# Gate and up products of a linear-attention block: another product carries a tail, other forms of x keep it, and W is loaded and summed in another order

## The chip, the cores and the metric

The kernel runs on one core of a Trainium2 chip. The metric is device time in microseconds, from launch to end, of one execution; lower is better. The engines are named as the profile names them: PE (matrix multiply) with PEld (its weight loads), DVE (vector), ACT (scalar, activation functions), POOL (gpsimd) and SP, which here only issues DMAs. Each engine runs its own instructions in program order, and so does each engine's DMA queue: a DMA that has to wait keeps back those behind it.

## The reference

One block of float32 work on x of 2048 rows and 576 columns: a layer norm, a linear attention with 32 heads, and a gated feed-forward of width 4608 that gates it.

```python
xn = layernorm(x)
s  = linear_attention(xn, wqkv) @ wo
g  = xn @ w_gate                     # 2048 x 4608
u  = xn @ w_up                       # 2048 x 4608
b  = (gelu(g) * u) @ w_down          # 2048 x 576
out = x + s * silu(b)
```

## The kernel before

All products are made from words: a float32 operand is cut into a high word (a rounding to `float32r`, made by a copy on ACT) and a low word (operand minus high word, made by a subtraction on DVE), and a product is the sum of three passes, high by high, high by low and low by high.

**Stages.** Keys and values of row tiles 0 to 7 (`kv_tile`) and the q products of the first half of x (`q_store`, to about 107 us), the same for tiles 8 to 15 and the second half (to about 220), the attention's output s (`s_mm`, to about 287), gate and up (`matrix`, to about 1087), and the down product (`down_all`, to the end). Work of one stage is prepared in the gaps of the stage before by lists of closures (`behind`, `ahead`, `aside`) that run after a numbered tile.

**Gate and up.** There are 36 matrices W of 576 x 256, gate and up in turn, each multiplied by all of x. Rows of x come in four blocks of 512 (two halves `s` of the sequence with two blocks `b` each), and W, without its last 64 of the 576 inputs, in 2 x 2 quarters of 256 x 128. A 2 x 2 product is made from seven products instead of eight, with sums of quarters of W (`S1` to `S4`, `mat_sums` on POOL) and of x (`T1` to `T4`, formed once). They come in this order, with the PSUM name that each adds into:

| number | 0 | 1 | 2 | 3 | 4 | 5 | 6 |
|---|---|---|---|---|---|---|---|
| PSUM | al | be | ga | de | al | ga | de |
| W | A11 | S2 | S1 | S3 | A12 | S4 | A22 |
| x | B11 | T2 | T1 | T3 | B21 | B22 | T4 |

The last 64 inputs are the *tail*. It isn't part of the scheme of seven: four products carry one plain tail product each, of 64 rows of W (`wtail`, cut from `raw[q][:, 4]`) with 64 rows of x that stand in slot 2 of a form of x. Before, they are number 3 (tail of T3), 4 (T1), 5 (T3) and 6 (T2, whose tail is that of block 0 minus that of block 1, so that what number 3 put into `de` is taken out again).

**Two halves of each product.** PE's rows are used as two groups of 64. The early half of a product pairs the lower 64 rows for `s = 1` with the upper 64 for `s = 0`, the late half the other way about. `step` (line 996) issues the early half of a product, then the sums and cuts that belong two products back (`post_0` to `post_6`, each followed by the list `todo[i]`), then the late half of the product before. So the order on PE is E0 L6 E1 L0 E2 L1 E3 L2 E4 L3 E5 L4 E6 L5, where L6 belongs to the matrix before. A half has 12 matmuls; a tail makes it 14 (early) or 16 (late). `act(seen ...)` reads a PSUM bank after each early half, which ties ACT's order to PE's. The rows of the profile call forms of x that were built in place for `s = 1` `xo_T`, `xo_B`, and those kept in HBM and loaded back for `s = 0` (`keep`, `back`) `xr_T`, `xr_B`.

**W.** `raw[q]` is one buffer (640 KB). In matrix q the words of matrix q + 1 are cut: A11 in `todo[0]`, S1 to S3 in `todo[3]`, A12, A22 and the tail in `todo[4]`, S4 in `todo[5]`; right behind the cuts of `todo[4]` SP is given the load of W of q + 2. `mat_sums(q + 1)` is given to POOL ahead of the whole matrix q.

**Results of gate and up.** Four matrices make a macro step of 28 hooks (`HOOKS`, one per product). Products land in 17 spots of SBUF; POOL adds them up by the hand-written table `ADDS` (sum, two terms, sign, hook), and finished ones are stored to HBM on SP one hook later (`put_out`; the last macro stores on POOL). A spot is used again once its store has landed. These run from `run_events`, the last entry of each `todo[i]`.

**The way into the down stage** is given by `down_first`, spread over the `todo` lists of the last matrix: loads of weights into the buffers `REG` ("22" into 13, "42" into 7), words of them (`w_head`, and `w_end` in 11), and loads of the first stored results (`raw_a` in buffer 15, which held the words `wa`, and `raw_b` in 10). Buffer 7 held T2 and 8 held T1 for `s = 0` (`X_BACK`), 11 T2 and 10 T3 for `s = 1` (`X_SLOT`).

**Forms of x.** `form("T1")`, `form_apart("T3")`, `form("T2")` and a begun `T4` make those for `s = 0` during the q products and the first tiles after them; `build` makes those for `s = 1` during `s_mm`. `tail` fills slot 2; for T2 it subtracts two blocks on DVE (`xd`), copies on ACT and subtracts on DVE, twice.

Of the kernel before, what the change touches and what calls it, by code (L numbers as in the profile page):

```python
# [8 lines left out]
F32 = mybir.dt.float32  # L9
# [7 lines left out]
P = 128  # L17
# [78 lines left out]
TAIL = {"T1": (0,), "T3": (1,), "T2": (0, 1)}  # L96
# [6 lines left out]
def block_kernel(ctx, tc, x, xe, xt, wq_d, wkv_d, wo, wgu_d, wd_d, out):  # L103
# [69 lines left out]
    small = sb.tile([P, 640], F32, name="small")  # L173
# [174 lines left out]
    def kept_words(nm, o):  # L348

        if nm in TAIL:  # L350
            return o.rearrange("p k t -> p (k t)")
        return bass.AP(
            tensor=o.tensor, offset=o.offset, ap=[list(o.ap[0]), [3 * TBN, 2], [1, 2 * TBN]]
        )

    def kept_place(nm, d):

        if nm in TAIL:
# [3 lines left out]
    def kept(s, nm):  # L362
        store[s, nm] = d = dr.tile(
            [P, 5 if nm in TAIL else 4, TBN], F32, name=f"kept_{s}_{nm}"
# [11 lines left out]
    def tail(s, nm, o):  # L376

        h = s * TR
        for j in range(2):
            vs = [xf[s][BS[b][j]][:, 2, :] for b in TAIL[nm]]  # L380
            r, low = (slice(i + j * KR, i + (j + 1) * KR) for i in (h, TR - h))
            v = vs[0][r]
            if len(vs) == 2:
                d = tmp([P, TBN], f"xd_{s}_{j}")
                vec("tensor_sub", d[r], v, vs[1][r])
                v = d[r]
            act(o[r], v, AF.Copy)
            vec("tensor_sub", o[low], v, o[r].bitcast(F32))
# [4 lines left out]
    def form_lo(s, nm, o):  # L393
        vec("tensor_sub", o[:, 3:5], xf[s][nm][:, 0:2], o[:, 0:2].bitcast(F32))
        if nm in TAIL and (s, nm) not in store:
            tail(s, nm, o[:, 2, :])

    def build(s, nm, i):
        xo[s][nm] = o = big(i, [P, 5, TBN], F32R, f"xo_{s}_{nm}")
# [516 lines left out]
    def mat_sums(q):  # L916
        if q >= NQ:
            return
        rv = raw[q][:, 0:4].rearrange("p (j k) (f c) -> p j f k c", j=2, f=2)
        a11, a21, a12, a22 = rv[:, 0, 0], rv[:, 0, 1], rv[:, 1, 0], rv[:, 1, 1]  # L920
        sm = mid(2, [P, 4, 2, P], F32, f"sm_{q}")
# [4 lines left out]
        sums[q] = rv, sm  # L926
# [6 lines left out]
    def cut_tail(q):  # L933
        o, src = wt["tail", q % 2], raw[q][:, 4, :]
# [9 lines left out]
    def mat_pieces(q):  # L944
# [3 lines left out]
        rv, sm = sums.pop(q)  # L948
        if q % 2 == 0:
            raws_ = [lambda: cut_w(wt["b"][:, 1:3], rv[:, 1])]  # L950
        else:
            raws_ = [
                lambda: cut_w(wt["b"][:, 1:2], rv[:, 1, 0:1]),
                lambda: cut_w(wt["b"][:, 0:1], rv[:, 1, 1:2]),
            ]
        raws_.append(lambda: cut_tail(q))
        return [
            [lambda: cut_w(wt["a"][:, 0:1], rv[:, 0, 0:1])],
            [], [],
            [lambda: cut_w(wt["a"][:, 1:4], sm[:, 0:3])],  # L960
            raws_,
            [lambda: cut_w(wt["b"][:, 3:4], sm[:, 3:4])],
# [52 lines left out]
    def matrix(q, c22, done, todo):  # L1015

        u, bs = {}, {}
        wtail = wt["tail", q % 2]

        def tail_of(f, nm):  # L1020
            c = slice(f * P, (f + 1) * P)
# [824 lines left out]
```

## Time and profile before

| | us |
|---|---|
| median of three runs | 1476.9 (1473.81 to 1477.27) |
| the profiled execution, its own time | 1477.23 |
| its span, first to last instruction | 1475.4 |
| mean granted clock of PE | 0.992 of full speed |

The profile is of that one execution. Its page gives busy times and the costliest groups; the trace behind it can be asked for waits (who stood still, and what ended it), for the chain of work that ended last, for a timeline of one engine and for windows. In a row "a<-b,c" the first name is what is written. "[2.56 <-DMA hs<-spot_h]" behind a row is the idle time ahead of it and what ended it. Ends of matmuls are modelled, and durations on POOL are rough.

### The profile page before, as it was taken

The numbers are of one execution on the slowest core, as the hardware profiler recorded it, in microseconds if no ns is written. First come the engines' busy times: TensorE is split into PE (matmuls) and PEld (weight loads), VectorE is DVE, ScalarE is ACT, GpSimd is POOL, SyncE is SP. The second block draws the span as 40 slices with busy tenths as digits, with TensorE's granted clock in tenths as the row PEclk, the third lists the DMA queues.
The fourth block names the chain that finished last, engine by engine and source line by source line (L and its number), as shares of the span: only waits on it lengthen the run. The fifth ranks groups of instructions, "written<-read, shape, count | busy, mean of one in ns | idle before, by whom it ended". The sixth has DMA issues, their size and how long they took to land.

```text
span 1475.4 us, 29114 instructions
## 1 busy us (share of the span) xinstructions
PE 1441.6 (98%) x11656; PEld 1299.7 (88%) x11656; DVE 993.8 (67%) x1491; ACT 574.5 (39%) x1217; POOL 515.5 (35%) x520
## 2 busy tenths in 40 slices
PE   9998999999999999999999999999979999999998
PEld 8988988999988788887888888888779999999998
DVE  7687667344665555566554565655658987989888
ACT  6444365333222332322333322333225546455454
POOL 3341340114564547556364664538423000000000
PEclk9999999999999999999999999999989999999999
DMA  5545105522323314324242332324169888767886
GB/s 221 174 164 168 44 10 177 189 101 80 134 100 108 122 57 155 101 90 143 66 144 76 136 104 103 128 75 145 68 224 350 280 254 258 237 189 240 278 287 218
DMA packets 120594, 228.68 MB, mean 155 GB/s; under 512 B 11690, under 2 KB 45386, under 8 KB 119690
## 3 DMA queue, kind: packets, MB, share of 16 engines
q1 hardware_dynamic: 117530, 214.82, 43.8%
q0 software_dynamic: 2784, 11.80, 2.2%
q8 instruction: 92, 1.51, 0.4%
q14 instruction: 44, 0.36, 0.1%
q10 hardware_dynamic: 144, 0.20, 0.0%
HBM read 145.20 MB, written 81.53 MB: 154 GB/s over the span
## 4 chain that ended last, share of the span: by engine, by line
PE 85%; DVE 6%; DMA 5%; ACT 2%; issue 1%; POOL 1%; SPq 0%; ACTq 0%; DVEq 0%; POOLq 0%
PE bd L152 23%; PE de L152 15%; PE al L152 13%; PE ga L152 13%; PE kv L152 8%; PE be L152 5%; PE s L152 3%; DMA hs<-spot_h 2%; PE q L152 2%; DVE wb L149 1%; PE kv_a L152 1%; DVE xo_T L149 1%; DMA xr_B<-kept_B 1%; DVE raw_h L149 0%; DVE sx L149 0%
## 5 line engine op out<-in xcount | busy, mean ns | idle before, releaser
L155 POOL TENSOR_TENSOR sm<-raw 128x256 f32<-128x256 f32 x72 | 53.1, 737 | 287.3 <-DMA raw<-in_wgu_dram 247.2
L152 PE MATMUL de<-xr_T,wa 64*128 64x512 f32 x540 | 140.7, 388 | 5.4 <-DVE spot_h L149 3.5
L152 PE MATMUL de<-xo_T,wa 64*128 64x512 f32 x540 | 141.9, 388 | 0.0
L152 PE MATMUL de<-xo_T,wb 64*128 64x512 f32 x540 | 139.7, 386 | 0.0
L152 PE MATMUL de<-xr_T,wb 64*128 64x512 f32 x540 | 139.7, 386 | 0.0
L152 PE MATMUL kv<-wkv,xo_B 128*128 128x412 f32 (+2 forms) x662 | 127.0, 351 | 4.8 <-ACT xo_B L146 4.8
L152 PE MATMUL ga<-xr_T,wa 64*128 64x512 f32 x486 | 127.7, 387 | 0.0
L152 PE MATMUL ga<-xo_T,wa 64*128 64x512 f32 x486 | 127.7, 387 | 0.0
L152 PEld LDWEIGHTS kv<-wkv,xo_B 128*128 128x128 f32 x662 | 121.8, 190 | 6.6 <-ACT xo_B L146 5.4
L152 PE MATMUL bd<-w_head,hi 128*128 128x288 f32 x516 | 119.3, 298 | 8.2 <-ACT hi L146 8.2
L149 DVE TENSOR_TENSOR wa<-raw,wa 128x256 fp32r<-128x256 f32 x54 | 43.1, 799 | 114.8 <-ACT wa L146 114.8
L152 PEld LDWEIGHTS de<-xr_T,wa 64*128 64x128 f32 x540 | 98.8, 184 | 16.6 <-DVE spot_h L149 6.0
L152 PE MATMUL ga<-xo_B,wb 64*128 64x512 f32 x432 | 110.1, 387 | 3.2 <-DVE spot_m L149 3.2
L152 PE MATMUL al<-xr_B,wb 64*128 64x512 f32 x432 | 110.6, 389 | 1.7 <-DMA xr_B<-kept_B 1.7
L152 PE MATMUL al<-xo_B,wb 64*128 64x512 f32 x432 | 110.6, 389 | 0.0
L152 PE MATMUL ga<-xr_B,wb 64*128 64x512 f32 x432 | 110.0, 388 | 0.1
L152 PE MATMUL al<-xr_B,wa 64*128 64x512 f32 x432 | 109.5, 386 | 0.0
L152 PE MATMUL al<-xo_B,wa 64*128 64x512 f32 x432 | 109.5, 386 | 0.0
L152 PE MATMUL be<-xr_T,wa 64*128 64x512 f32 x432 | 109.4, 386 | 0.0
L152 PE MATMUL be<-xo_T,wa 64*128 64x512 f32 x432 | 109.4, 386 | 0.0
L152 PEld LDWEIGHTS de<-xo_T,wb 64*128 64x128 f32 x540 | 99.4, 184 | 9.4
L152 PEld LDWEIGHTS de<-xo_T,wa 64*128 64x128 f32 x540 | 98.8, 184 | 9.6
(297 smaller groups left out, 4596.1 us busy)
## 6 DMA issues: line engine op xcount, KB each, us to landing
raw_h<-hs SPq DMA_DIRECT2D x176, 256.0 KB
raw<-in_wgu_dram SPq DMA_DIRECT2D x36, 640.0 KB
hs<-spot_h SPq DMA_DIRECT2D x90, 256.0 KB
hs<-spot_g SPq DMA_DIRECT2D x80, 256.0 KB
b<-in_wd_dram SPq DMA_DIRECT2D x42, 432.0 KB
hs<-spot_m SPq DMA_DIRECT2D x38, 256.0 KB
raw_g<-hs SPq DMA_DIRECT2D x22, 256.0 KB
raw_a<-hs SPq DMA_DIRECT2D x20, 256.0 KB
```

The lines of the kernel that those rows point to most:

```text
L149: pin(getattr(nc.vector, op)(*args, **kw))
L152: pin(nc.tensor.matmul(*args, **kw))
L155: pin(getattr(nc.gpsimd, op)(*args, **kw))
```

## The change

Tails: number 2 (`ga`, S1 with T1) now carries the second half of the W tail with block 1's tail of x, number 3 carries none, number 4 the first half with block 0's tail, number 5 the difference of the two W halves with block 1's, and number 6 the second half with block 0's. All are plain tails of x; the difference is now on the side of W: `mat_sums` makes one more subtraction on POOL (128 x 128), and `cut_two` cuts it into two words (`wt["last"]`, in the buffer that `small` had). Block 0's tail is kept in T4 for both halves of the sequence; block 1's in T1 (`s = 0`) and T3 (`s = 1`). So T4 and T1 are now stored and loaded with five slots for `s = 0`, and T2 and T3 with four.

Order: `mat_sums(q + 1)` moves from ahead of matrix q to the head of `todo[0]`, its sums live in one lasting tile, and the load of W of q + 2 moves from the end of the cuts in `todo[4]` to the end of `todo[5]`, behind that list's events. At the start B21 is loaded back ahead of W of matrix 1 instead of behind it. For `s = 1` block 0's tail is made beside T1 as before, but into T4, whose buffer is opened earlier.

```diff
@@ -93,7 +93,7 @@
 
 MAIN = ((0, 0), (0, 2), (2, 0), (1, 1), (1, 3), (3, 1))
 XW = (0, 1, 3, 4)
-TAIL = {"T1": (0,), "T3": (1,), "T2": (0, 1)}
+TAIL = ({"T4": 0, "T1": 1}, {"T4": 0, "T3": 1})
 TR = P // 2
 
 X_SLOT = {"B11": 0, "B21": 1, "B22": 3, "T1": 9, "T3": 10, "T2": 11, "T4": 2}
@@ -170,7 +170,7 @@
     ident = sb.tile([P, P], F32, name="ident")
     make_identity(nc, ident)
     eps_t, zx, seen = eps_t[:, 0:1], eps_t[:, 2:3], eps_t[:, 4:6]
-    small = sb.tile([P, 640], F32, name="small")
+    small = sb.tile([P, 640], F32, tag="small", bufs=1, name="small")
     nc.gpsimd.memset(eps_t, LN_EPS)
 
 
@@ -347,7 +347,7 @@
 
     def kept_words(nm, o):
 
-        if nm in TAIL:
+        if nm in TAIL[0]:
             return o.rearrange("p k t -> p (k t)")
         return bass.AP(
             tensor=o.tensor, offset=o.offset, ap=[list(o.ap[0]), [3 * TBN, 2], [1, 2 * TBN]]
@@ -355,13 +355,13 @@
 
     def kept_place(nm, d):
 
-        if nm in TAIL:
+        if nm in TAIL[0]:
             return d.rearrange("p k t -> p (k t)")
         return d.rearrange("p (a b) t -> p a (b t)", a=2)
 
     def kept(s, nm):
         store[s, nm] = d = dr.tile(
-            [P, 5 if nm in TAIL else 4, TBN], F32, name=f"kept_{s}_{nm}"
+            [P, 5 if nm in TAIL[0] else 4, TBN], F32, name=f"kept_{s}_{nm}"
         )
         return d
 
@@ -373,30 +373,30 @@
         d = kept(s, nm)
         dma(out=kept_place(nm, d), in_=kept_words(nm, o.bitcast(F32)))
 
-    def tail(s, nm, o):
+    def tail(s, b, o):
 
         h = s * TR
         for j in range(2):
-            vs = [xf[s][BS[b][j]][:, 2, :] for b in TAIL[nm]]
+            v = xf[s][BS[b][j]][:, 2, :]
             r, low = (slice(i + j * KR, i + (j + 1) * KR) for i in (h, TR - h))
-            v = vs[0][r]
-            if len(vs) == 2:
-                d = tmp([P, TBN], f"xd_{s}_{j}")
-                vec("tensor_sub", d[r], v, vs[1][r])
-                v = d[r]
-            act(o[r], v, AF.Copy)
-            vec("tensor_sub", o[low], v, o[r].bitcast(F32))
+            act(o[r], v[r], AF.Copy)
+            vec("tensor_sub", o[low], v[r], o[r].bitcast(F32))
 
     def form_hi(s, nm, o):
         act(o[:, 0:2], xf[s][nm][:, 0:2], AF.Copy)
 
     def form_lo(s, nm, o):
         vec("tensor_sub", o[:, 3:5], xf[s][nm][:, 0:2], o[:, 0:2].bitcast(F32))
-        if nm in TAIL and (s, nm) not in store:
-            tail(s, nm, o[:, 2, :])
+        if nm in TAIL[s] and nm != "T4":
+            tail(s, TAIL[s][nm], o[:, 2, :])
+
+    def begin(s, nm, i):
+        xo[s][nm] = big(i, [P, 5, TBN], F32R, f"xo_{s}_{nm}")
 
     def build(s, nm, i):
-        xo[s][nm] = o = big(i, [P, 5, TBN], F32R, f"xo_{s}_{nm}")
+        if nm not in xo[s]:
+            begin(s, nm, i)
+        o = xo[s][nm]
         form_hi(s, nm, o)
         form_lo(s, nm, o)
         return o
@@ -916,14 +916,21 @@
     def mat_sums(q):
         if q >= NQ:
             return
-        rv = raw[q][:, 0:4].rearrange("p (j k) (f c) -> p j f k c", j=2, f=2)
+        rv = quarters(q)
         a11, a21, a12, a22 = rv[:, 0, 0], rv[:, 0, 1], rv[:, 1, 0], rv[:, 1, 1]
-        sm = mid(2, [P, 4, 2, P], F32, f"sm_{q}")
+        if not sums:
+            t = mid(2, [P, 9, P], F32, "sums")
+            sums["sm"] = t[:, 0:8].rearrange("p (s f) c -> p s f c", f=2)
+            sums["last"] = t[:, 8]
+        sm = sums["sm"]
         pool("tensor_add", sm[:, 0], a21, a22)
         pool("tensor_sub", sm[:, 1], sm[:, 0], a11)
         pool("tensor_sub", sm[:, 2], a11, a21)
         pool("tensor_sub", sm[:, 3], a12, sm[:, 1])
-        sums[q] = rv, sm
+        pool("tensor_sub", sums["last"], raw[q][:, 4, 0:P], raw[q][:, 4, P:])
+
+    def quarters(q):
+        return raw[q][:, 0:4].rearrange("p (j k) (f c) -> p j f k c", j=2, f=2)
 
     def cut_w(o, src):
 
@@ -931,7 +938,9 @@
         vec("tensor_sub", o[:, :, 2:4, :], src, o[:, :, 0:2, :].bitcast(F32))
 
     def cut_tail(q):
-        o, src = wt["tail", q % 2], raw[q][:, 4, :]
+        cut_two(wt["tail", q % 2], raw[q][:, 4, :])
+
+    def cut_two(o, src):
         act(o[:, 0], src, AF.Copy)
         vec("tensor_sub", o[:, 1], src, o[:, 0].bitcast(F32))
 
@@ -945,21 +954,25 @@
 
         if q >= NQ:
             return [[] for _ in range(7)]
-        rv, sm = sums.pop(q)
-        if q % 2 == 0:
-            raws_ = [lambda: cut_w(wt["b"][:, 1:3], rv[:, 1])]
-        else:
-            raws_ = [
-                lambda: cut_w(wt["b"][:, 1:2], rv[:, 1, 0:1]),
-                lambda: cut_w(wt["b"][:, 0:1], rv[:, 1, 1:2]),
-            ]
-        raws_.append(lambda: cut_tail(q))
+
+        def raws_(q=q):
+            rv = quarters(q)
+            if q % 2 == 0:
+                cut_w(wt["b"][:, 1:3], rv[:, 1])
+            else:
+                cut_w(wt["b"][:, 1:2], rv[:, 1, 0:1])
+                cut_w(wt["b"][:, 0:1], rv[:, 1, 1:2])
+            cut_tail(q)
+
         return [
-            [lambda: cut_w(wt["a"][:, 0:1], rv[:, 0, 0:1])],
+            [lambda: cut_w(wt["a"][:, 0:1], quarters(q)[:, 0, 0:1])],
             [], [],
-            [lambda: cut_w(wt["a"][:, 1:4], sm[:, 0:3])],
-            raws_,
-            [lambda: cut_w(wt["b"][:, 3:4], sm[:, 3:4])],
+            [lambda: cut_w(wt["a"][:, 1:4], sums["sm"][:, 0:3])],
+            [raws_],
+            [
+                lambda: cut_w(wt["b"][:, 3:4], sums["sm"][:, 3:4]),
+                lambda: cut_two(wt["last"], sums["last"]),
+            ],
             [],
         ]
 
@@ -1015,11 +1028,11 @@
     def matrix(q, c22, done, todo):
 
         u, bs = {}, {}
-        wtail = wt["tail", q % 2]
-
-        def tail_of(f, nm):
-            c = slice(f * P, (f + 1) * P)
-            return [(wtail[:, :, c], X[s][nm][:, 2, :]) for s in range(2)]
+        w1, w2 = (wt["tail", q % 2][:, :, f * P : (f + 1) * P] for f in range(2))
+
+        def tail_of(w, b):
+            at_ = [next(nm for nm, c in TAIL[s].items() if c == b) for s in range(2)]
+            return [(w, X[s][at_[s]][:, 2, :]) for s in range(2)]
 
         def both(bk, wn, xn, start, post, tail_=None):
             if start:
@@ -1070,11 +1083,11 @@
 
         both("al", "A11", "B11", True, post_0)
         both("be", "S2", "T2", True, post_1)
-        both("ga", "S1", "T1", True, post_2)
-        both("de", "S3", "T3", True, post_3, tail_of(1, "T3"))
-        both("al", "A12", "B21", False, post_4, tail_of(0, "T1"))
-        both("ga", "S4", "B22", False, post_5, tail_of(0, "T3"))
-        both("de", "A22", "T4", False, post_6, tail_of(1, "T2"))
+        both("ga", "S1", "T1", True, post_2, tail_of(w2, 1))
+        both("de", "S3", "T3", True, post_3)
+        both("al", "A12", "B21", False, post_4, tail_of(w1, 0))
+        both("ga", "S4", "B22", False, post_5, tail_of(wt["last"], 1))
+        both("de", "A22", "T4", False, post_6, tail_of(w2, 0))
 
     DONE = {(1, 1): 3, (0, 0): 4, (0, 1): 5, (1, 0): 6}
     HOOKS = 28
@@ -1672,12 +1685,10 @@
         hi, lo, last = (slot([P, 2, TBN], F32R, f"xo_0_{nm}_{i}") for i in range(3))
         act(hi, f[:, 0:2], AF.Copy)
         vec("tensor_sub", lo, f[:, 0:2], hi.bitcast(F32))
-        for i, nm_ in enumerate((nm, "T2")):
-            tail(0, nm_, last[:, i])
+        tail(0, TAIL[0]["T4"], last[:, 0])
         dma(out=d[:, 0:2], in_=hi.bitcast(F32))
-        dma(out=d[:, 3:5], in_=lo.bitcast(F32))
-        for i, d in enumerate((d, kept(0, "T2"))):
-            dma(out=d[:, 2], in_=last[:, i].bitcast(F32))
+        dma(out=d[:, 2:4], in_=lo.bitcast(F32))
+        dma(out=kept(0, "T4")[:, 2], in_=last[:, 0].bitcast(F32))
 
     behind = {
         (0, 0): [
@@ -1743,7 +1754,10 @@
 
     q_load(0, 7)
     aside = {
-        (2, 0): [lambda: den(3), lambda: build(1, "T1", X_SLOT["T1"])],
+        (2, 0): [
+            lambda: den(3), lambda: build(1, "T1", X_SLOT["T1"]), lambda: begin(1, "T4", X_SLOT["T4"]),
+            lambda: tail(1, 0, xo[1]["T4"][:, 2, :]),
+        ],
         (2, 1): [lambda: scale(3, 0, 1), lambda: halve(3, 0, 1)],
         (2, 2): [lambda: scale(3, 2, 3, 4), lambda: halve(3, 2, 3, 4)],
         (2, 3): [lambda: build(1, "T3", X_SLOT["T3"]), lambda: load_mat(0), lambda: q_load(1, 8)],
@@ -1764,23 +1778,25 @@
             s_mm(tb, t)
             run(aside.get((tb, t), []))
     w_tile("b", 14)
+    wt["last"] = sb.tile([P, 2, P], F32R, tag="small", bufs=1, name="w_last")
     back("T3")
     run(pieces[4] + pieces[5])
+    back("B21", eng=nc.sync)
     load_mat(1)
-    back("B21", "B22", "T4", eng=nc.sync)
+    back("B22", "T4", eng=nc.sync)
     open_spots()
     for q in range(NQ):
         g = q // 2
         if q % 4 == 0:
             open_macro(q // 4)
-        mat_sums(q + 1)
         todo = mat_pieces(q + 1)
-        todo[4].append(lambda q=q: load_mat(q + 2))
+        todo[0].insert(0, lambda q=q: mat_sums(q + 1))
         if q == NQ - 1:
             for a, b in zip(todo, down_first()):
                 a += b
         for i in range(7):
             todo[i].append(lambda at=7 * q + i: run_events(at))
+        todo[5].append(lambda q=q: load_mat(q + 2))
         (gate_matrix if q % 2 == 0 else up_matrix)(g, todo)
     flush()
     down_all()
```

## The prediction

> **What bounds the kernel now.** I read the page first, then the waits of PE, then the clock in windows around them, then the chain of waits. The page gives the execution that all sums below are made against:
>
> ```profile
> span 1475.4 us, 29114 instructions
> PE 1441.6 (98%) x11656; PEld 1299.7 (88%) x11656; DVE 993.8 (67%) x1491; ACT 574.5 (39%) x1217; POOL 515.5 (35%) x520
> ```
>
> That execution took 1477.2 us, 0.3 over the median of 1476.9. PE is busy almost throughout, so an edit pays only where PE stands still, or runs slowly because it stood still. The waits of PE (total, times, longest):
>
> ```profile
> PE bd L152 <- ACT hi L146: 8.2, 1, 8.2
> PE kv L152 <- ACT xo_B L146: 4.8, 1, 4.8
> ...
> PE ga L152 <- DVE spot_m L149: 3.2, 1, 3.2
> PE al L152 <- DMA xr_B<-kept_B: 1.7, 1, 1.7
> ...
> PE b L152 <- ACT s L146: 1.0, 1, 1.0
> PE s L152 <- ACT s L146: 0.6, 1, 0.6
> ```
>
> Each belongs to another place, and the change touches all of them. (The rows left out are PE's waits for spots, which the chain shows below.) Three are followed by a slow clock (window, its length, busy time of PE, PEld, DVE, ACT, POOL, granted clock, DMA share, GB/s):
>
> ```profile
> 119.75:123.70 3.95, 3.95 (x11) 3.78 (x12) 1.95 (x6) 2.48 (x7) 1.31 (x1) 0.50 0.94 305
> 250.10:253.40 3.30, 3.30 (x14) 3.30 (x15) 3.30 (x6) 2.05 (x4) 0.00 (x0) 0.50 0.98 345
> 1055.60:1058.90 3.30, 3.30 (x18) 2.59 (x16) 0.12 (x1) 1.67 (x4) 1.74 (x3) 0.50 0.25 99
> ```
>
> At 0.50 half of a busy stretch is lost: 2.0, 1.65 and 1.65 us, on top of the waits ahead of them.
>
> **The change part by part.** I write E3 and L3 for the early and late half of the fourth product (fifth: E4, L4, and so on).
>
> *PE's own work: nothing.* A plain tail adds two pairs' worth of matmuls in the late half and one in the early; four products have one before and after. It moves from `de` to `ga` within E2 to L3, whose sum stays.
>
> *New work, hidden.* Per matrix one subtraction on POOL and one copy on ACT and one subtraction on DVE, all 128x128. Nearest rows, for twice the width:
>
> ```profile
> L155 POOL TENSOR_TENSOR sm<-raw 128x256 f32<-128x256 f32 x72 | 53.1, 737 | 287.3 <-DMA raw<-in_wgu_dram 247.2 <-DVE spot_h L149 31.6 <-DVE spot_m L149 8.5
> L149 DVE TENSOR_TENSOR wb<-sm,wb 128x256 fp32r<-128x256 f32 x36 | 15.2, 423 | 18.1 <-ACT wb L146 18.1
> L146 ACT ACTIVATE wb<-sm 128x256 fp32r<-128x256 f32 x36 | 14.6, 406 | 0.0
> ```
>
> So each lies between 0 and 0.74, 0.42 and 0.41 us; I take the upper ends. POOL stood idle 287 us ahead of these very sums, and DVE and ACT have a third or more of the span free. At the place where the DVE one is added (sixth product) the next reader is the seventh product's sum, and PE needs that bank only at E3 of the next matrix. If that cover were gone it would cost 36 x 0.42 = 15 us.
>
> *A, forms of x, first half: 6.4 gained.* T2 had its tail formed from a difference, in ping-pong between DVE and ACT. DVE's timeline, the PE row after it, and the same for the second half:
>
> ```profile
> 98.43 0.68 DVE L149 TENSOR_TENSOR xd<-xf_B,xf_B 32x512 f32<-32x512 f32 x1
> ...
> 102.62 0.69 DVE L149 TENSOR_SCALAR ph<-q 128x512 f32<-128x512 f32 x1
> ```
>
> ```profile
> 119.75 12.45 PE L152 MATMUL kv<-wkv,xo_B 128*128 128x416 f32 x56 [4.82 <-ACT xo_B L146]
> ```
>
> ```profile
> 243.59 0.69 DVE L149 TENSOR_TENSOR xd<-xf_B,xf_B 32x512 f32<-32x512 f32 x1
> ...
> 247.78 1.28 DVE L149 TENSOR_TENSOR ph<-ph,b 128x512 f32<-128x512 f32 x2
> ```
>
> From 98.43 to 102.62 DVE does only this: 4.2 us. The chain runs from there through DVE and ACT to the `xo_B` for which PE waits 4.82 us. What else could be late there, the q products, runs without a gap, so 4.2 to 4.8 goes; I take 4.4, and the 2.0 of slow clock with it. Bounds: 0, if ACT is late by itself, to 6.8.
>
> *B, second half: 3.3 gained.* The same 4.2 us of T2's tail hold ACT, whose copies of s then come late; PE waits 1.0 and 0.6, then loses 1.65 to the slow clock. What is late next is `scale`'s product, ready 4 us earlier. Bounds: 0 to 3.3. T1's tail becomes T4's in the same place: nothing.
>
> *C, first matrix: 3.2 lost.* The kept form with a tail is now T4, which is loaded last, and E4 reads its tail; before, T4 was first read in E6. The chain here, and a window after the loads:
>
> ```profile
> 290.21 9.04 DMA xr_B<-kept_B
> ...
> 299.39 1.83 PE al L152 x13
> ```
>
> ```profile
> 300.00:302.30 2.30, 2.30 (x24) 2.29 (x22) 0.34 (x1) 0.17 (x1) 0.00 (x0) 1.00 1.00 410
> 302.50:304.50 2.00, 2.00 (x21) 2.00 (x19) 1.28 (x2) 0.00 (x0) 0.00 (x0) 1.00 0.05 20
> ```
>
> E4 waited until 299.39 for B21, 1.7 us. B21 now goes ahead of the W load on SP, so that wait goes. But all loads together end at about 302.3, at 410 GB/s with every DMA engine busy, and the bytes are the same (T3 lost the piece that T4 gained). PE does E4's twelve plain matmuls (1.36 us) from 297.7 and waits from 299.0 to about 302.2: 3.2 us, 1.5 more than before. The nearest wait of that length, 3.2 at `ga`, was followed by 1.65 us of slow clock; I take that too. Bounds: 0 to 8.
>
> The Trainium skill (TensorE: Matmul & The Clock Gate, Why this matters for your kernels) tells kernels to have no idle gaps over some 3 us between bursts, and says in its Part 1 that it takes an idle window of about 3.4 us to halve the clock. By that the wait of 3.2 might keep its clock and C would be 1.5. The row at 250 us disagrees: 1.6 us in two pieces were enough there.
>
> *E, one wait per macro: 7.9 gained.* The chain:
>
> ```profile
> 301.22 1.81 PE de L152 x16
> ...
> 322.98 1.81 PE de L152 x16
> ...
> 399.76 5.31 DMA hs<-spot_h
> ...
> 1027.17 1.81 PE de L152 x16
> ```
>
> The three PE rows are L3 of matrices 0, 1 and 33. A matrix takes 21.76 us; 33 of them are 718.1, but 725.95 passed: 7.9 us lost in eight places, where `de` of the matrix that follows a macro's first waits for DVE, and DVE for a spot whose store lands late. SP's, POOL's and DVE's timelines at the first place:
>
> ```profile
> 399.33 0.33 SPq L158 DMA_DIRECT2D raw<-in_wgu_dram  x1
> ```
>
> ```profile
> 391.37 2.54 POOL L155 TENSOR_TENSOR spot_h<-spot_g,spot_h 128x512 f32<-128x512 f32 x2
> ...
> 397.20 1.48 POOL L155 TENSOR_TENSOR spot_h<-spot_h,spot_h 128x512 f32<-128x512 f32 x1
> 404.49 0.73 POOL L155 TENSOR_TENSOR sm<-raw 128x256 f32<-128x256 f32 x1 [5.81 <-DMA raw<-in_wgu_dram]
> ```
>
> ```profile
> 405.09 0.69 DVE L149 TENSOR_TENSOR spot_h<-u,de 128x512 f32<-128x512 f32 x1 [2.56 <-DMA hs<-spot_h]
> ```
>
> The value to be stored was ready on POOL at 393.9. Its store stands on SP behind the W load, which waits for the cuts of the W before it until 399.3; so it left at 399.76 and landed 5.3 us later. With the load behind the sixth product's events the store can leave at about 394 and land by 399.5, and DVE, which lacked 2.56 us, has it in time. POOL too is no longer held at `sm` ahead of its adds. The W load keeps its time as long as the two stores now ahead of it are ready before 399.3; the last of their adds ends at 398.7 already, and POOL's are to come earlier. If that failed, each us that W comes late is free up to the bound in the last but one rival.
>
> *D, the last macro: 4.9 gained.* `ga` waits 3.2 us for `spot_m`, behind this:
>
> ```profile
> 1044.62 7.51 DVE L149 TENSOR_TENSOR wa<-raw,wa 128x256 fp32r<-128x256 f32 x1 [2.88 <-ACT wa L146]
> ```
>
> The group it belongs to:
>
> ```profile
> L149 DVE TENSOR_TENSOR wa<-raw,wa 128x256 fp32r<-128x256 f32 x54 | 43.1, 799 | 114.8 <-ACT wa L146 114.8
> ```
>
> The other 53 mean 0.67; this one lies across a row of POOL adds, backed up because POOL waited for W. With the first adds ahead of that wait I expect the collision gone: 3.2 and 1.65 of clock. Bounds: 0 to 4.9.
>
> *F, the way into the down stage: 8.7 gained.* SP's timeline, the chain, ACT's and DVE's:
>
> ```profile
> 1068.99 18.05 SPq L158 DMA_DIRECT2D b<-in_wd_dram  x2
> 1087.13 2.30 SPq L158 DMA_DIRECT2D raw_a<-hs  x4
> ```
>
> ```profile
> 1076.41 1.81 PE de L152 x16
> ...
> 1085.02 1.83 PE de L152 x16
> ```
>
> ```profile
> 1086.87 1.16 ACT L146 ACTIVATE w_end<-b 128x1152 fp32r<-128x1152 f32 x1 [3.39 <-PE de L152]
> ```
>
> ```profile
> 1095.05 1.23 DVE L149 TENSOR_TENSOR raw_a<-raw_a,hi 128x1024 fp32r<-128x1024 f32 x1 [5.63 <-ACT hi L146]
> ```
>
> The second `b` load overwrites T2 of the first half (buffer 7), and `w_end` T2 of the second (buffer 11). T2's tail was the last thing that L6 read (1085.02 to 1086.85), so both, and `raw_a` behind the load on SP, came after it. Now T2 is last read in L1. `raw_a` then waits only for `wa`, free when L3 ends at 1078.2: 8.9 us earlier. ACT's word copy no longer waits, and DVE's low word starts at about 1086.2, 8.9 earlier. PE can go on at 1086.9 instead of 1095.1, but now waits at times for DVE, so I take DVE's shift less 0.2. Bounds: 4.4 (if `raw_b` counts: its T3 is read until L5's end at 1085.0, and before it left behind `raw_a` at 1089.4) to 8.9.
>
> Sum: 6.4 + 3.3 - 3.2 + 7.9 + 4.9 + 8.7 = 28.0; 1477.2 - 28.0 = **1449.2**.
>
> **The rivals.**
> - *DVE is caught behind POOL again* at 1044: the sums and the cut of the same W now start on the same landing. For: POOL has the same adds and one more operation. Against: in the other macros the cut got in after one POOL operation. D is lost: 1454.1. The Trainium skill (SBUF — State Buffer, SBUF: two separate sides) says that whichever of the two engines starts first keeps the shared pair for its whole instruction, so a wait would end with one POOL operation. The 7.51 us row, against adds of 1.3, is longer than that.
> - *The down stage starts only on what L5 frees:* F falls to 4.4: 1453.5. Against: `raw_b` is the third unit, DVE reaches it late.
> - *The stores stay late,* because POOL's adds and not SP are what counts: E and D fall away: 1462.0. Against: 393.9 beside 399.76.
> - *W comes late, slower.* The load now stands behind stores that wait for POOL's adds, and those stand behind sums that wait for W. D's row shows from where it decides: that cut of W ended at 1052.1 and cost 3.2, so an end at 1048.9 was free, 3.9 us after that of an undisturbed one (1044.62 and 0.42). If W landed 5 us later than the cut asks for it, in every matrix, 35 x 1.1 = 38.5 us are lost and D and E with them: 1477.2 - 15.2 + 38.5 = 1500.5.
> - *The clock holds in C:* 1447.5.
>
> **How the numbers follow.** The forecast 0.56, DVE caught 0.15, L5 0.10, stores late 0.08, W late 0.03, the clock held 0.08. The unknowns of A, C and F widen the forecast to 1444 to 1453; with the rivals that cost 5 us and part of the next, 1443.5 to 1459. About 0.3% (4.4 us) is what a measurement can tell from no change: faster 0.95, within 0.02, slower 0.03.
>
> **What would show it.** A: no wait of `kv` at 115 and no 0.50 there. B: none of `b` and `s` at 246. C: PE's wait at the first `al` names xr_T. E: L3 to L3 at 21.76 across macros, and `hs` stores ahead of each `raw` load on SP. D: no `wa<-raw` over 2 us. F: `raw_a` issued at L3's end. Wrong it is if POOL's `sm` still waits at the head of its adds, if new waits for `wa` or `raw` stand in each matrix, or if DVE's longer row ahead of the seventh product reaches PE.

## The result and the profile after

Before: 1475.67 us, median of four runs (1473.81 to 1477.27). After: **1452.28 us**, median of four runs (1451.9 to 1454.09). The ratio is 0.9844, with a 95% interval of 0.9827 to 0.9861. The profiled execution of after took 1454.09 us by its own time, 23.1 less than that of before. Its page:

```profile
span 1452.4 us, 29230 instructions
...
PE 1435.6 (99%) x11656; PEld 1361.9 (94%) x11656; DVE 1006.7 (69%) x1519; ACT 578.2 (40%) x1249; POOL 542.7 (37%) x556
```

POOL has 36 instructions more, DVE 28, ACT 32: the new pieces of work, less the tails of T2. PE has as many as before. What stood between its matmuls is what changed. The waits of PE (total, times, longest), after:

```profile
PE al L152 <- DMA xr_T<-kept_T: 5.3, 1, 5.3
PE ga L152 <- DVE spot_m L149: 2.2, 1, 2.2
...
PE bd L152 <- DVE raw_b L149: 1.1, 1, 1.1
```

Gone are `hi` (8.2), `xo_B` (4.8), the two of s at 246 and every wait of `de`. `ga` is left with 2.2 of its 3.2. Two waits are new: `al` for `xr_T`, which is large, and `bd` for `raw_b`.

The two traces compared at fixed points of PE's order (the start of the same matmul in both) give each step its share. A runs to the first q product of the second half (its first 80 us, with the same code in both, are counted under start and end), B from there to E0 of the first matrix, C to E0 of the second, E to E0 of the 35th, D to E0 of the 36th, F to the 73rd matmul of the down stage.

| step | forecast, gain in us | measured |
|---|---|---|
| A | 6.4 | 6.3 |
| B | 3.3 | 4.5 |
| C | -3.2 | -6.5 |
| E | 7.9 | 7.8 |
| D | 4.9 | 1.3 |
| F | 8.7 | 9.1 |
| start and end of the kernel | 0 | 0.5 |
| sum | 28.0 | 23.0 |

The 5 us between forecast and result come from C and D, which fell short by 6.9; B, F and the two ends gave 2.1 more than forecast. **C** first: SP's timeline and the chain after.

```profile
278.15 0.61 SPq L158 DMA_DIRECT2D xr_B<-kept_B  x1
...
280.49 0.57 SPq L158 DMA_DIRECT2D xr_T<-kept_T  x1
```

```profile
280.49 13.81 DMA xr_T<-kept_T
...
294.35 0.79 PE al L152
```

And the windows there (window, length, busy PE, PEld, DVE, ACT, POOL, granted clock, DMA share, GB/s):

```profile
289.00:291.00 2.00, 0.09 (x2) 0.00 (x0) 1.62 (x3) 0.41 (x2) 1.92 (x3) 1.00 1.07 451
291.00:292.00 1.00, 0.00 (x0) 0.00 (x0) 1.00 (x3) 0.00 (x0) 1.00 (x3) 1.00 0.99 420
292.00:292.50 0.50, 0.00 (x0) 0.00 (x0) 0.39 (x1) 0.00 (x0) 0.36 (x1) 1.00 0.21 82
292.50:294.00 1.50, 0.00 (x0) 0.00 (x0) 0.00 (x0) 0.00 (x0) 0.00 (x0) 0.91 0.05 20
294.00:294.30 0.30, 0.00 (x0) 0.00 (x0) 0.00 (x0) 0.00 (x0) 0.00 (x0) 0.50 0.00 0
...
297.00:300.00 3.00, 3.00 (x16) 2.34 (x14) 1.29 (x2) 0.00 (x0) 0.00 (x0) 0.50 0.00 0
```

B21 is no longer waited for, as forecast, and T4, issued last, is. The burst of loads ends at about 292, 15 us after E0 of the first matrix at 276.97; before, that was also about 15 (287.40 to 302.3). But a thin rest runs on until 294.0: 20 GB/s at a share of 0.05, which is about one of the 16 DMA engines (1/16 is 0.06). The load counts as landed at 294.30, when that rest is through, some 2 us after the burst.

**D**: DVE's cut of `wa`, POOL's row of adds beside it, and the window behind the wait, after.

```profile
1033.05 6.26 DVE L149 TENSOR_TENSOR wa<-raw,wa 128x256 fp32r<-128x256 f32 x1 [1.99 <-ACT wa L146]
```

```profile
1032.16 1.30 POOL L155 TENSOR_TENSOR spot_h<-spot_h,spot_h 128x512 f32<-128x512 f32 x1
...
1037.14 0.56 POOL L158 DMA_DIRECT2D hs<-spot_h  x1
1037.72 1.29 POOL L155 TENSOR_TENSOR spot_h<-spot_h,spot_g 128x512 f32<-128x512 f32 x1
1039.10 1.34 POOL L155 TENSOR_TENSOR spot_g<-spot_h,spot_g 128x512 f32<-128x512 f32 x1
```

```profile
1041.20:1044.60 3.40, 3.40 (x15) 2.44 (x17) 1.70 (x3) 0.00 (x0) 3.30 (x4) 0.51 0.38 154
```

The cut is caught again, for 6.26 us instead of 7.51; it ends with the fifth add of the row, as it did before.

### The profile page after: what moved, and what is told of

The parts are those of the page before. It is cut to its first block, busy times and chain, and to the rows that moved or that the text cites. A ratio compares the mean times of both kernels' runs of the same rounds, so it can differ in the third digit from the quotient of the medians.

```text
span 1452.4 us, 29230 instructions
## 1 busy us (share of the span) xinstructions
PE 1435.6 (99%) x11656; PEld 1361.9 (94%) x11656; DVE 1006.7 (69%) x1519; ACT 578.2 (40%) x1249; POOL 542.7 (37%) x556
## 4 chain that ended last, share of the span: by engine, by line
PE 89%; DVE 5%; DMA 2%; issue 1%; ACT 1%; SPq 0%; POOL 0%; ACTq 0%; DVEq 0%; POOLq 0%
PE bd L152 21%; PE ga L152 17%; PE de L152 15%; PE al L152 15%; PE kv L152 7%; PE be L152 6%; PE s L152 4%; PE q L152 2%; DMA raw_h<-hs 1%; DMA xr_T<-kept_T 1%; PE kv_a L152 1%; DVE raw_h L149 1%; DVE xo_T L149 1%; DVE wa L149 0%; DVE sx L149 0%
## 5 line engine op out<-in xcount | busy, mean ns | idle before, releaser
L155 POOL TENSOR_TENSOR sums<-raw 128x256 f32<-128x256 f32 (+1 forms) x108 | 70.4, 652 | 165.0 <-DMA raw<-in_wgu_dram 124.0
L152 PE MATMUL de<-xr_T,wa 64*128 64x512 f32 x486 | 128.8, 389 | 0.0
L152 PE MATMUL de<-xo_T,wa 64*128 64x512 f32 x486 | 128.6, 389 | 0.0
L152 PE MATMUL de<-xo_T,wb 64*128 64x512 f32 x486 | 121.6, 386 | 0.0
L152 PE MATMUL ga<-xo_T,wa 64*128 64x512 f32 x486 | 121.6, 386 | 0.0
L152 PE MATMUL de<-xr_T,wb 64*128 64x512 f32 x486 | 121.6, 386 | 0.0
L152 PE MATMUL ga<-xr_T,wa 64*128 64x512 f32 x486 | 121.6, 386 | 0.0
L146 ACT ACTIVATE hi<-raw_h 128x1024 fp32r<-128x1024 f32 x59 | 62.4, 1059 | 86.1 <-PE bd L152 58.0
L152 PEld LDWEIGHTS de<-xo_T,wa 64*128 64x128 f32 x486 | 90.3, 186 | 4.0
L152 PEld LDWEIGHTS de<-xr_T,wa 64*128 64x128 f32 x486 | 90.1, 186 | 3.1
```

Of the source, the lines that this page charges most:

```text
L146: pin(nc.scalar.activation(*args, **kw))
L152: pin(nc.tensor.matmul(*args, **kw))
L155: pin(getattr(nc.gpsimd, op)(*args, **kw))
```

## The experiments

Each is one execution unless it says otherwise, its trace compared with that of after (or of before) at the same fixed points. Up to the 73rd matmul of the down stage, kernels with the same code at a place differ there by under 0.8 us, except in C and D, where the slow clock falls differently: C cost 5.0 to 6.5 with the code of after, and D took 1.8 less to 0.7 more in other executions of the code of before than in its own profile.

**Load of W back in its old place.**

```diff
+        todo[4].append(lambda q=q: load_mat(q + 2))
...
-        todo[5].append(lambda q=q: load_mat(q + 2))
```

> The changed kernel with one move undone: the load of W of q + 2 stands again behind the cuts in the fifth list, ahead of that list's stores. Theory (SP's order made E): the stores leave behind the load again, eight waits of de for a spot come back, matrix 1 to matrix 33 takes 7.8 us more, 1460.1. Rival (POOL's order made E, since the sums no longer stand ahead of the adds): the sums stay where the change put them, so no wait comes back, 1452.3.

It took 1472.06 us. The macros cost 21.3 us more than in after: eight waits of `de` of 1.6 to 2.5 us are 15.7 of it, and behind two of them, at 583 and 942 us, the clock also stood at 0.50 for 3.4 us. SP's timeline, then DVE's:

```profile
396.34 0.33 SPq L158 DMA_DIRECT2D raw<-in_wgu_dram  x1
396.76 0.38 SPq L158 DMA_DIRECT2D hs<-spot_h  x1
```

```profile
392.15 4.16 DVE L149 TENSOR_TENSOR wb<-raw,wb 128x256 fp32r<-128x256 f32 x3 [1.38 <-ACT wb L146]
...
402.08 0.69 DVE L149 TENSOR_TENSOR spot_h<-u,de 128x512 f32<-128x512 f32 x1 [2.35 <-DMA hs<-spot_h]
```

The store leaves right behind the load, and DVE waits for it: SP's order is the cause of these waits. The loss is larger than the 7.9 of before. POOL's adds, which no longer stand behind the sums of the W to come, lie over the cuts that the load waits for (by POOL's timeline from 390.0 to 396.0 without a gap), and three cuts take 4.16 us, where before had

```profile
396.66 2.64 DVE L149 TENSOR_TENSOR wb<-raw,wb 128x256 fp32r<-128x256 f32 x3 [1.94 <-ACT wb L146]
```

**Load and sums both back.** As above, with `mat_sums(q + 1)` ahead of the matrix and a tile of sums of its own for each.

```diff
+        mat_sums(q + 1)
         todo = mat_pieces(q + 1)
-        todo[0].insert(0, lambda q=q: mat_sums(q + 1))
+        todo[4].append(lambda q=q: load_mat(q + 2))
```

> The changed kernel with both moves undone: the load as in the run before and the sums of q + 1 given to POOL ahead of matrix q again, in a tile of their own for each q. Theory (SP's order): the same 7.8 us as with the load alone, 1460. Rival (POOL's order): nothing with the load alone and 7.8 us here.

1463.57 us: 9.5 more than after in the macros, near the 7.9 that before lost, in eight waits of 0.5 to 1.7 us. `ga` waits 3.5 behind a cut of 7.54 us. So the two moves pay together; that of the sums alone (the kernel above) costs 12 us against neither. The load's move alone, with the sums in their old place, was not run, so how much of the 7.9 it would bring by itself is not shown.

**T4's tail loaded apart, early.** E4 reads slot 2 of T4 and no other.

```diff
     back("B21", eng=nc.sync)
+    X[0]["T4"] = big(X_BACK["T4"], [P, 5, TBN], F32R, "xr_T4")
+    dma(X[0]["T4"][:, 2].bitcast(F32), store[0, "T4"][:, 2])
     load_mat(1)
-    back("B22", "T4", eng=nc.sync)
+    back("B22", eng=nc.sync)
+    for k in (0, 3):
+        dma(X[0]["T4"][:, k : k + 2].bitcast(F32), store[0, "T4"][:, k : k + 2])
```

> The changed kernel with slot 2 of T4 loaded by a DMA of its own (256 KB) right behind B21, and the other four slots last, as two DMAs. Theory (E4 waits for T4 only because its tail lands with the last of 5 MB): the wait of 5.25 us and the 6.8 us of half clock behind it (3.4 us) go, 1452.3 - 8.6 = 1443.7. Rival (the burst of loads is what takes long): the wait moves on to E5, which reads B22, or to the words of W of matrix 1, and half or more of it stays, 1448 or more.

1445.07 us, with C 5.8 less than in after. Waits of PE:

```profile
PE ga L152 <- DVE spot_m L149: 2.2, 1, 2.2
...
PE de L152 <- ACT eps_t L146: 0.8, 1, 0.8
PE ga L152 <- DVE spot_h L149: 0.7, 1, 0.7
```

The 5.3 of `al` and the slow clock behind it are gone, so it was the landing of T4 as a whole that E4 waited for, and nothing else of the loads. At D the wait of 2.2 stands as in after, but the granted clock stays at 1.00 there, and that alone makes 1.4.

**The last macro's stores on SP.**

```diff
-        eng = nc.gpsimd if m == NM - 1 else nc.sync
+        eng = nc.gpsimd if m == NM - 1 and at >= HOOKS * m + 20 else nc.sync
```

> The changed kernel with the last macro's stores up to its hook 19 on SP's queue instead of POOL's. Theory (DVE's subtraction of 6.3 us is caught because POOL issues stores between its adds): that row falls to about 1.4 us as in the other macros, ga's wait of 2.2 us and the half clock behind it (1.65 us) go, 1448.4. Rival (the row of back-to-back adds alone catches DVE): the row stays at 5 us or more and the time at 1452.3.

1447.45 us, D 4.4 less than in after, no wait of `ga`. The same cut, then POOL's adds:

```profile
1031.21 1.38 DVE L149 TENSOR_TENSOR wa<-raw,wa 128x256 fp32r<-128x256 f32 x1 [1.99 <-ACT wa L146]
```

```profile
1031.02 1.29 POOL L155 TENSOR_TENSOR spot_g<-spot_g,spot_h 128x512 f32<-128x512 f32 x1
1032.27 1.48 POOL L155 TENSOR_TENSOR spot_h<-spot_h,spot_h 128x512 f32<-128x512 f32 x1
```

The cut starts inside the row and gets in behind one add. So the collision needs POOL's stores; by what they make it, the next run asks. (Without them the row also starts earlier against the cut, 1.45 us ahead of it instead of 0.89. That isn't what frees the cut: in the run below with the new work in the first matrix alone the row starts 1.37 us ahead, with POOL's stores, and the cut is caught.)

**Only the store in the middle of the row on SP.**

```diff
-        eng = nc.gpsimd if m == NM - 1 else nc.sync
+        eng = nc.gpsimd if m == NM - 1 and v != 38 else nc.sync
```

> The kernel after, with one store of the last macro on SP's queue instead of POOL's: the one that POOL issues at 1037.14, in the middle of its row of adds. The cut of wa starts at 1033.05 as in after, with POOL's first add already running; so the place where the row is broken by a DMA issue is all that changes. Theory one, DVE is let in only at POOL's next DMA issue: the cut holds to the one that follows, two adds later, 8 to 10 us instead of 6.26, ga waits 4 to 6 us and the time is 1454 to 1459. Theory two, the number of adds or the phase decides, not the DMA: 6.26 again (1452.3), or 1.4 and no wait of ga (1447.5).

1453.5 us. DVE's cut, POOL's row and a window behind the wait:

```profile
1032.97 5.70 DVE L149 TENSOR_TENSOR wa<-raw,wa 128x256 fp32r<-128x256 f32 x1 [1.99 <-ACT wa L146]
```

```profile
1037.08 1.29 POOL L155 TENSOR_TENSOR spot_h<-spot_h,spot_g 128x512 f32<-128x512 f32 x1
...
1039.74 0.56 POOL L158 DMA_DIRECT2D hs<-spot_h  x1
```

```profile
1042.00:1044.00 2.00, 2.00 (x12) 1.51 (x12) 0.25 (x1) 0.00 (x0) 1.87 (x3) 0.50 0.16 64
```

Theory one falls: DVE is released at 1038.67, ahead of POOL's next DMA. It is again the end of the fifth add, now 0.56 us earlier because no DMA stands ahead of it. Theory two is nearer: the same add decides, though neither of its two times came. Why the fifth, and why the cut got in behind one add in the kernel with all early stores on SP, stays open. One store was in every execution in which the cut was caught, the one that POOL issues right ahead of the row; it was not moved by itself.

**Before, with one line moved:** the load of weights "42" behind `raw_a`.

```diff
-            [lambda: load_reg("42", "42")],
+            [],
...
-            [lambda: load_reg("32", "32"), lambda: cut(1)],
+            [lambda: load_reg("42", "42"), lambda: load_reg("32", "32"), lambda: cut(1)],
```

> The kernel before, with one line moved: the load of weights into buffer 7 ("42") is issued in todo[5] of the last matrix instead of todo[1], so that SP can issue raw_a ahead of it. T2 is still read last in L6, so ACT's word copy into buffer 11 still waits for L6. My theory, that two waits stand one behind the other in F (SP's queue, then ACT's and DVE's words): raw_a leaves at L3's end, hi goes on as soon as w_end is through, and of the 9.1 us of F some 5.7 are gained: about 1470. Rival one, SP's queue alone: the whole 8.7 to 9.1, about 1467. Rival two, ACT's w_end alone: nothing, 1475.7.

1468.74 us; of F 5.7 are gained, and D came 1.8 lighter, with the same code. SP's timeline (the moved load leaves at 1085.22) and ACT's:

```profile
1075.64 1.76 SPq L158 DMA_DIRECT2D raw_a<-hs  x4
```

```profile
1084.71 1.16 ACT L146 ACTIVATE w_end<-b 128x1152 fp32r<-128x1152 f32 x1 [3.40 <-PE de L152]
1085.78 1.99 ACT L146 ACTIVATE hi<-raw_a 128x1024 fp32r<-128x1024 f32 x2
```

`raw_a` leaves early and ACT still waits for L6: two waits, one behind the other, as the forecast of F had them.

**Before, without T2's tail.** It leaves out the difference of two blocks in the seventh product; PE's work is the same.

```diff
-TAIL = {"T1": (0,), "T3": (1,), "T2": (0, 1)}
+TAIL = {"T1": (0,), "T3": (1,)}
...
-        both("de", "A22", "T4", False, post_6, tail_of(1, "T2"))
+        both("de", "A22", "T4", False, post_6, tail_of(1, "T3"))
```

> The kernel before, without T2's tail: none is formed for either half, and product 6 takes the tail of T3 in the place of T2's. It leaves out the difference of two blocks in the tail of the seventh product, so PE's work is the same and the output isn't the reference's. My theory: A, B and F all hang on T2's tail alone (two of them on forming it, one on its last reader), so the wait of kv at 115, those of b and s at 246 and of hi at 1087 go, with the clock behind them: -6.3 -4.5 -9.1, about 1455.8; no step in C, D or E. Rival: A and B came from other things that the change moves (T4's buffer opened earlier, other stores of the forms), so only F goes: 1466.6.

1459.65 us. A gains 6.3 and B 4.5, C nothing, E no more than other executions of the same code differ (0.4), and the 73rd matmul of the down stage comes 9.0 earlier. So A, B and F are T2's tail and nothing else of the change. Some 4 us go again behind that point, with a new wait of `hi` for a load of `raw_a`, which after doesn't have:

```profile
PE bd L152 <- ACT hi L146: 1.4, 1, 1.4
```

**The new work four times, for every matrix.** The subtraction on POOL, the copy on ACT and the subtraction on DVE.

```diff
+        for _ in range(4):
-        pool("tensor_sub", sums["last"], raw[q][:, 4, 0:P], raw[q][:, 4, P:])
+            pool("tensor_sub", sums["last"], raw[q][:, 4, 0:P], raw[q][:, 4, P:])
...
-                lambda: cut_two(wt["last"], sums["last"]),
+                *[lambda: cut_two(wt["last"], sums["last"])] * 4,
```

> The kernel after, with the new subtraction on POOL, the new copy on ACT and the new subtraction on DVE issued four times per matrix instead of once (the same values are written again). My theory, that this work lies under PE: 1452.3, give or take 2. Rival, that the new work is on PE's path in each matrix: three more subtractions on DVE of up to 0.42 us cost up to 36 x 1.26 = 45 us, so up to 1497, and a part of the new work is then in the time of after too.

1474.93 us: 27 more in the macros, some of it won back in C and D. Neither theory's number. Which engine has so little room, and whether after pays already, is for the next three. **POOL's subtraction alone fourfold:**

```diff
+        for _ in range(4):
-        pool("tensor_sub", sums["last"], raw[q][:, 4, 0:P], raw[q][:, 4, P:])
+            pool("tensor_sub", sums["last"], raw[q][:, 4, 0:P], raw[q][:, 4, P:])
```

> The kernel after, with only the new subtraction on POOL issued four times per matrix; the copy and subtraction of its two words once. With all three fourfold the kernel took 22 us more, in macro steps of about 2.7 us: two waits of de of some 0.5 and one of be of 1.2. Theory one, POOL is the engine whose cover is thin: its adds come 3 x 0.46 = 1.4 us later in each matrix, DVE's cuts lie under them again (4.3 us for three) and the spots come late, so the two waits of de stay, 8 x 1.0, some 8 to 14 us more than after: 1460 to 1466, with no wait of be. Theory two, ACT and DVE are the thin ones: nothing, 1452.3.

1448.33 us, with nothing lost in the macros: theory one falls, POOL has room. It is even faster than after, by 4.4 in D. The cut starts 0.4 us earlier than in after, as all does there, but POOL's row 1.2 later, and the cut is through ahead of it:

```profile
1032.63 0.51 DVE L149 TENSOR_TENSOR wa<-raw,wa 128x256 fp32r<-128x256 f32 x1 [1.99 <-ACT wa L146]
```

```profile
1032.79 0.57 POOL L158 DMA_DIRECT2D hs<-spot_g  x1
1033.39 1.30 POOL L155 TENSOR_TENSOR spot_h<-spot_h,spot_h 128x512 f32<-128x512 f32 x1
```

**The copy and DVE's subtraction alone fourfold,** copies first:

```diff
+                *[lambda: act(wt["last"][:, 0], sums["last"], AF.Copy)] * 3,
                 lambda: cut_two(wt["last"], sums["last"]),
+                *[lambda: vec("tensor_sub", wt["last"][:, 1], sums["last"], wt["last"][:, 0].bitcast(F32))] * 3,
```

> The kernel after, with only the copy on ACT and the subtraction on DVE fourfold, the copies ahead of the subtractions so that the two engines don't wait for each other in between; POOL's subtraction once. Theory one (POOL is thin): no waits of de; ACT reads the bank of be 0.9 us later, which PE notices only if less is free there; 1452 to 1460. Theory two (ACT and DVE are thin): waits of be and de in each macro or each matrix, 1465 to 1475.

1462.92 us: 14.8 more in the macros, where PE's weight loads wait:

```profile
PEld de L152 <- DVE spot_h L149: 12.2, 19, 1.0
```

The thin cover is DVE's (and ACT's ahead of it): behind these subtractions DVE's queue holds the reads of the bank of `de`, and some two us later is too late (401.11 at the first place, 399.07 in after). The two apart give 14.8 and not 27; all three together also let copies and subtractions alternate, and what the rest hangs on isn't shown.

**The new work in the first matrix alone.** It leaves out the tail difference of W from the second matrix on.

```diff
+        if q == 0:
-        pool("tensor_sub", sums["last"], raw[q][:, 4, 0:P], raw[q][:, 4, P:])
+            pool("tensor_sub", sums["last"], raw[q][:, 4, 0:P], raw[q][:, 4, P:])
...
-                lambda: cut_two(wt["last"], sums["last"]),
+                *([lambda: cut_two(wt["last"], sums["last"])] if q == 0 else []),
```

> The kernel after, with the new subtraction, copy and subtraction done in the first matrix alone; it leaves out the tail difference of W from the second matrix on (the old words are used again). PE's work is the same. My theory, that the new work costs nothing as it stands in after: 1452.3, give or take 1, and the macros keep their 21.76 us per matrix. Rival, that after already pays for it somewhere: lower by what it pays, at most 36 x 0.4 = 14 us (1438), and that in the steps of the macros or in the last one.

1449.29 us, and no macro is shorter: E is the same to 0.01 us. Of the 4.8 us less than in the profile of after, C has 1.5 and D 1.8, the two places with a slow clock, which lasted less long in C and didn't come in D; the rest is the start and the end. In D the wait is 1.7 instead of 2.2: POOL's row starts without the added subtraction ahead of it, so there after pays about 0.5 us. In the macros the new work costs nothing. POOL's store and first adds, and DVE's cut:

```profile
1029.42 0.57 POOL L158 DMA_DIRECT2D hs<-spot_g  x1
1030.01 1.30 POOL L155 TENSOR_TENSOR spot_h<-spot_h,spot_h 128x512 f32<-128x512 f32 x1
1031.25 1.30 POOL L155 TENSOR_TENSOR spot_g<-spot_g,spot_h 128x512 f32<-128x512 f32 x1
```

```profile
1031.38 5.78 DVE L149 TENSOR_TENSOR wa<-raw,wa 128x256 fp32r<-128x256 f32 x1 [3.10 <-ACT wa L146]
```

This cut starts 0.13 us behind the second add, the one with the early stores on SP 0.19 behind it: nearly the same place in the row, 5.78 against 1.38. So POOL's stores make the difference, and not the place.

**After, with both places mended** (T4's tail apart, early stores of the last macro on SP), timed in five rounds:

> The kernel after, with both places mended where it fell short of the forecast: T4's tail loaded by its own DMA right behind B21, the rest of T4 last in two pieces, and the last macro's stores up to its hook 19 on SP's queue instead of POOL's. My theory, that the two are apart (one at the first matrix, one in the last macro) and add up: 1445.1 - 4.4 = 1440.7, a ratio of 0.976 to before. Rival: the half clock of one place is paid anyway somewhere behind it, and the sum stays at 1445.

**1441.94 us**, median of five (1440.63 to 1442.93); the ratio to before is 0.9768, interval 0.9755 to 0.9781. C is 6.1 and D 4.4 less than in after, so the two add up. All waits of PE of 0.3 us or more behind its first 10 us:

```profile
PE bd L152 <- DVE raw_b L149: 1.0, 1, 1.0
PE ga L152 <- DVE spot_h L149: 0.7, 1, 0.7
PE de L152 <- ACT eps_t L146: 0.7, 1, 0.7
PE bd L152 <- DVE raw_a L149: 0.4, 1, 0.4
```

## Why the prediction was right, and where its sum was off

The forecast was 1449.2 and the median of after is 1452.28, within the range of 1443.5 to 1459. The mechanisms were those named, except at D, where a rival that had a chance of 0.15 came true; and the sizes at B, which gained more, and at C, which lost more, were off.

- **PE's own work and the new work: nothing.** Right but for some 0.5 us in the last macro, shown by leaving it out. The forecast named POOL's and DVE's idle time as its cover; on DVE that cover is smaller than the share of idle time suggests: three more copies and subtractions cost 14.8 us.
- **A, 6.4: right** (6.3), by the run without T2's tail.
- **B, 3.3: the mechanism right, the size low** (4.5, and 4.5 without T2's tail). The sum took the two waits for s and the slow clock; it left out 0.3 of waits for `ph` between them. The remaining 0.9 lies at the same place: from the matmul at 247.51 to the fourth behind it, at 250.08, PE takes 2.57 us where after takes 0.83, and only 0.86 of that difference is recorded as waits.
- **C, 3.2 lost: the wait right, its size half of what came** (6.5). It read the landing of the last load off the end of the burst, "at about 302.2". The burst did end as early as it assumed, but about one DMA engine ran on until 294.0, the landing came behind that at 294.30, and PE waited 5.25 instead of 3.2. The forecast's own row for 302.50 to 304.50 has the same thin rest before the change, 20 GB/s at a share of 0.05. Why one engine has more left than the others isn't shown. And the price of the slow clock came from one wait with 1.65 behind it; here the 0.50 lasted 6.8 us in the windows of the clock, twice as long. 5.25 less 1.7 for the old wait, and some 3 for the clock, is about the 6.5 measured. The bounds, 0 to 8, held it.
- **D, 4.9: it failed** (1.3). "With the first adds ahead of that wait I expect the collision gone" was wrong; the rival with DVE caught again was right. Both the cut and the row of adds follow the same landing of W, and moving the sums only shifted one against the other. The cut takes 0.51 where it starts ahead of the store that POOL issues in front of the row (POOL's subtraction fourfold), and 0.42 in a pause between that store and the row (the copy and DVE's subtraction alone fourfold). Inside the store or the row it takes 5.7 to 7.5, and inside the row 1.38 with the early stores on SP. The 7.51 of before, which started at 1044.62, is one that started ahead of the first add, during the store:

```profile
1044.44 0.56 POOL L158 DMA_DIRECT2D hs<-spot_g  x1 [0.30 <-POOL spot_g L155]
1045.01 1.30 POOL L155 TENSOR_TENSOR spot_h<-spot_h,spot_h 128x512 f32<-128x512 f32 x1
```

The other macros have the adds without POOL's stores, which would explain why the forecast's argument from them didn't carry over.
- **E, 7.9: right** (7.8). Putting the load back brought the waits back with the store held behind it on SP, as forecast. What the forecast missed is how the two moves hang together: with the sums moved and the load not, the macros lose 21 us against after.
- **F, 8.7: right** (9.1). `raw_a` leaves at L3's end, at 1065.20 in after:

```profile
1065.20 1.76 SPq L158 DMA_DIRECT2D raw_a<-hs  x4
1072.00 1.74 SPq L158 DMA_DIRECT2D raw_b<-hs  x4
```

The rival in which `raw_b` counts was wrong: it does leave only at L5's end, and PE waits 1.1 for its word, inside the first 73 matmuls. That F is two waits in a row, SP's and ACT's, is shown by the moved line, which gave 5.7 of it.

- **Stores late, W late:** neither came. Stores stand ahead of the load of W on SP, and no macro waits:

```profile
389.88 0.32 SPq L158 DMA_DIRECT2D hs<-spot_h  x1
396.36 0.33 SPq L158 DMA_DIRECT2D raw<-in_wgu_dram  x1
```

## What to carry to other kernels

Ask of each buffer that a later stage takes over which read of it comes last, and what stands behind the DMA that waits for that read in its queue: A, B and F, 20 of the 29 us gained, came from one small operand that was dropped, its readers served from elsewhere. When the last transfer of a burst becomes one that is waited for, count from a landing in the trace and not from the end of the burst, since one engine may run on, and load the part that is read first by itself. Work that is queued ahead of a read of a PSUM bank has only that read's slack as its cover, whatever the engine's share of idle time is.

## What the runs showed of the hardware

**A load lands with the last of its DMA engines, not with the burst.** In the windows of C, DMA moves 420 GB/s up to 292, and then 20 GB/s at a share of 0.05, about one engine of 16, up to 294.0; the load counts as landed at 294.30. Before the change the row for 302.50 to 304.50 has the same rest. The Trainium skill (DMA: Bandwidth & Descriptors, Anatomy of one DMA — SWDGE (gpsimd) path) puts most of a fixed cost of about 2.0 us into the receipt of the last write. The section is about POOL's DMAs and this one was SP's; here some 0.3 us lie between the end of the traffic and the landing.

**Below some 3 us the length of a wait doesn't tell whether the clock halves.** In these traces every wait of PE of 3.1 us or more came with a stretch at 0.50; with shorter ones it went either way. At the same place, D, a wait of 2.2 us was followed by 3.4 us at 0.51 in after and by none in the kernel with T4's tail apart (mean granted clock 1.000); one of 1.6 by at least 2 us at 0.50 (the store in the middle on SP), and one of 3.0 by none (one line of before moved), whose windows behind the wait are

```profile
1053.40:1055.40 2.00, 1.88 (x13) 1.35 (x15) 1.76 (x3) 0.00 (x0) 1.98 (x3) 1.00 0.65 262
1055.40:1057.40 2.00, 2.00 (x22) 1.65 (x20) 0.00 (x0) 1.41 (x4) 1.39 (x2) 1.00 0.03 12
```

The Trainium skill (TensorE: Matmul & The Clock Gate, Part 1) has a window of about 3.4 us that runs freely and does not start with the kernel, and halves the clock after at least one idle window. Stretches of 3.4 us and, in C, of about twice that, and the same wait falling both ways, fit it; the 1.6 us, which is less than half a window, does not.

**A DVE subtraction can stand behind more than one POOL add.** The Trainium skill (SBUF — State Buffer, SBUF: two separate sides) lets the one that comes second wait for one instruction. That fits the 1.38 us with the stores on SP; 7.51, 6.26, 5.78 and 5.70 us, each up to the fifth add of a row, do not fit it, and the first of them had even started 0.39 us ahead of the row's first add.
